# Decoding fp64 weight words by their bits, with the order of the decode's steps and one sum of every third pair placed on other engines

## The chip, the cores and the metric

The kernel runs on one core of one Trainium2 chip. The metric is the device time of one execution in microseconds; times that are compared are medians of several executions. Five queues matter: TensorE (PE, with its weight loads PEld), VectorE (DVE), ScalarE (ACT), GpSimd (POOL) and SyncE (SP), which issues nearly all DMAs. Each works through its own instructions in program order and waits at the head of its queue.

## What is computed

The reference, cut to what matters (12480 rows, 128 columns):

```python
h_filt = (np.maximum(pos_emb @ w1, 0) @ w2) * np.exp(-0.01 * pos)[:, None]
u = x * v
y = np.fft.irfft(np.fft.rfft(u, n=2 * S, axis=1) * np.fft.rfft(h_filt, n=2 * S, axis=0), n=2 * S, axis=1)[:, :S]
x = x * y
x = relu(x @ w_in) ** 2 @ w_out          # 128 -> 2048 -> 128
h = x @ w_in2
x = where(h > 0, h, exp(min(h, 0)) - 1) @ w_out2
```

The four weight matrices come as fp64 words. The kernel loads them as pairs of 32-bit words and makes fp32 numbers of them on the chip, each then split into a high part (fp32r) and the rest, since the matmuls of the last stage are done as three fp32r products.

## The kernel before

The program has three stages. **Stage one** (to 83 us of the profiled execution) makes the filter and the first of two transform steps. **Stage two** (`phase2`, 83 to 220 us) walks over 46 pairs p = 0 to 45 of transform rows. **Stage three** (`phase3`, from 220 us on) runs the two feed-forward layers over 25 column tiles, with 12 matmuls of 512 columns at a time.

A pair p of stage two goes through these steps, written in program order by the loop over p at the end of `phase2`:

- `s2(p)`: four matmul records on PE into the tile u (L503). There are two u buffers in PSUM.
- `prod(p)`: the complex product of u with the filter tile hh. VectorE makes the two product tiles (L515 into pt, L516 into m2). GpSimd makes the difference (L518, in place in pt) and the sum (L519, from m2 into pt). For p >= 43 (`PD - 1`) VectorE makes both.
- `s2r` on even p (L362, tile rt, copied to rr by ACT) and `hmm` on odd p (L375, tile h, copied to hh by ACT): the filter's part for later pairs. `hmm` reads rr, `prod` reads hh.
- `ia(p - 2)`: two matmul records on PE from pt into v (L526), an ACT copy into z, and a DMA of z to DRAM. It therefore waits for GpSimd's sum of the pair two before.

The weights are decoded beside this by a generator, `weights`, that is advanced four times per pair (once for p = 0). There are 16 chunks c of 128 x 512 words. `decode(c)` issues an instruction or nothing at each advance; a decode starts no earlier than advance 10 c (`WDEC`) and only when the one before has ended. It has nine advances before: bits of the mantissa (L417) and of the exponent (L419) on VectorE, three ACT conversions (L422, L424, L426), the low word added in (L428) and the sign put in (L430) on VectorE, and a 128 x 512 product of mantissa and power of two on GpSimd (L436). After L430 the DMA of chunk c + 2 into the same raw buffer is issued on SP. `split(c)`, at least four advances after its decode, copies the word to fp32r on ACT (L168, `m<-wf`) and subtracts on GpSimd (L165, `m<-wf,m`).

At the end of stage two, `head` makes the first column tile. For p = 44 and 45 it uses pt directly (L580), then needs the z rows of all earlier pairs. The z rows of pairs 40 to 43 are copied one by one by SP (`z0`, L537); VectorE copies and combines them (L583, L658), PE multiplies (L638, which waits for L583), and the first matmul of stage three follows.

Of the kernel before, what the change touches and what calls it, by code (L numbers as in the profile page):

```python
# [10 lines left out]
F32 = mybir.dt.float32  # L11
F32R = mybir.dt.float32r
U32 = mybir.dt.uint32
AF = mybir.ActivationFunctionType
ALU = mybir.AluOpType
SYNC = mybir.DependencyInfo(mybir.DependencyClass.Sync, mybir.DependencyReason.DATA)
# [25 lines left out]
PD = NP - 2  # L42
# [2 lines left out]
KD = K1 - 2 * PD  # L45
WDEC = 10
OFF = 3
LO0 = 8
LAG1 = 2
NX = 10  # L50
# [9 lines left out]
def _tiles():  # L60
    seq = [(p, s) for p in range(CEN + 1) for s in (1, -1) if p or s == 1]
    out = []
    b = 0
    for g in SIZES:
        part = seq[b:b + g]
        right = [p for p, s in part if s == 1]
        left = [p for p, s in part if s == -1]
        if not out:
            part = [(p, 1) for p in right] + [(p, -1) for p in left]
        out.append((right, left, [R if s < 0 and CEN - p < SPLIT else R - 1 for p, s in part], part))  # L70
        b += g
    assert b == len(seq)
    return out


def _fill():
    tl = _tiles()
    left = sum(tl[NT][2])
    out, b = [], 0
    for t in range(NT):  # L80
        n = 0 if t < FILL else min(FULL - sum(tl[t][2]), left - b)
        out.append((b, b + n))
        b += n
    assert b == left
    return out
# [69 lines left out]
class Build:  # L155
# [11 lines left out]
    def copy(self, out, in_):  # L167
        self.nc.scalar.activation(out=out, in_=in_, func=AF.Copy)  # L168

    def setup(self):  # L170
        nc = self.nc
        const = self.const = self.pool("const")
        self.dram = self.pool("dram", 1, DRAM)
        self.zero = const.tile([128, 128], F32, name="zero")
        nc.vector.memset(self.zero, 0.0)
        self.ebias = const.tile([128, 3], F32, name="ebias")
        self.sg = const.tile([128, 3], F32, name="sg")
        nc.vector.memset(self.ebias[:, 0:1], 1151.0)
        nc.vector.memset(self.ebias[:, 1:2], 255.0 * 8388608.0)
        self.Z = self.dram.tile([K1, 128, 2 * D], F32, name="Zd")  # L180
        self.wp = self.pool("wp")
        self.tiles = _tiles()
        self.fill = _fill()
        self.st = {}
# [30 lines left out]
    def phase1(self):  # L215
        nc, a = self.nc, self.a
        with ExitStack() as ctx1:
# [58 lines left out]
            def zstep(s):  # L276
                f = fb[s % 2]
                for c in range(2):
# [11 lines left out]
                    for h in range(2):  # L290
                        for n in range(4):
                            nc.scalar.activation(out=f[:, 0, h, n], in_=z[:, h, n], func=AF.Relu,
                                                 scale=win[:, s, 0, h, n:n + 1])
# [105 lines left out]
    def load_weights(self, c):  # L399
        l, k, q = c // 8, c // 4 % 2, c % 4  # L400
        raw = self.buf("raw", [4, D, 2], 2, U32, self.p2b)
        src = self.a[(("moe_w_in", "moe_w_out"), ("moe2_w_in", "moe2_w_out"))[l][k]].bitcast(U32)
        if k == 0:
# [6 lines left out]
    def decode(self, c):  # L410
        nc = self.nc
        raw = self.raw.pop(c)
        low, high = raw[:, :, :, 0], raw[:, :, :, 1]
        e = self.buf("we", [4, D], 2, U32, self.p2b)
        f = self.buf("wf", [4, D], WF, pool=self.p2b)
        t, s, w, m = e.bitcast(F32), e, f, f.bitcast(U32)
        nc.vector.tensor_scalar(out=m, in0=high, scalar1=0xFFFFF, scalar2=None, op0=ALU.bitwise_and)  # L417
        yield
        nc.vector.tensor_scalar(out=e, in0=high, scalar1=1, scalar2=21,  # L419
                                op0=ALU.logical_shift_left, op1=ALU.logical_shift_right)  # L420
        yield
        nc.scalar.activation(out=f, in_=m, func=AF.Copy, scale=2.0 ** -20, bias=1.0)  # L422
        yield
        nc.scalar.activation(out=t, in_=e, func=AF.Relu, bias=self.ebias[:, 0:1], scale=-1.0)  # L424
        yield
        nc.scalar.activation(out=e, in_=t, func=AF.Relu, bias=self.ebias[:, 1:2], scale=-8388608.0)  # L426
        yield
        nc.vector.scalar_tensor_tensor(out=f, in0=low, scalar=2.0 ** -52, in1=f, op0=ALU.mult, op1=ALU.add)  # L428
        yield
        nc.vector.scalar_tensor_tensor(out=s, in0=high, scalar=0x80000000, in1=e,  # L430
                                       op0=ALU.bitwise_and, op1=ALU.bitwise_or)
        if c + 2 < 16:
            self.load_weights(c + 2)
        yield
        yield
        nc.gpsimd.tensor_tensor(out=w, in0=f, in1=s.bitcast(F32), op=ALU.mult)  # L436
        yield
        self.dec[c] = w

# [36 lines left out]
    def phase2(self):  # L476
        nc, a, st = self.nc, self.a, self.st
        ctx0 = self.ctx
        with ExitStack() as self.ctx:
# [29 lines left out]
            def prod(p):  # L509
                nj = self.nj(p)  # L510
                u = st.pop(("u", p))[:, :nj]
                h = st.pop(("h", p))[:, :nj]
                pt = m1 = self.buf("pt", [2, 2, D], 5, pool=p2b)[:N2, :nj]
                m2 = self.buf("m2", [2, 2, D], 2, pool=p2b)[:N2, :nj]
                nc.vector.tensor_tensor(out=m1, in0=u, in1=h, op=ALU.mult)  # L515
                nc.vector.tensor_tensor(out=m2, in0=u, in1=h[:, :, ::-1], op=ALU.mult)  # L516
                eng = nc.vector if p >= PD - 1 else nc.gpsimd
                eng.tensor_tensor(out=pt[:, :, 0], in0=m1[:, :, 0], in1=m1[:, :, 1], op=ALU.subtract)  # L518
                eng.tensor_tensor(out=pt[:, :, 1], in0=m2[:, :, 0], in1=m2[:, :, 1], op=ALU.add)  # L519
                st["p", p] = pt  # L520

# [74 lines left out]
            for p in range(NP):  # L596
                self.pair = p
                if p in HD:
                    next(hd)
                if p < PD:  # L600
                    s2(p)
                if p:
                    next(wgen, None)
                prod(p)
                if p % 2 == 0 and p + 2 < NP:
                    self.s2r(p // 2 + 1)
                if p:
                    next(wgen, None)
                if p % 2 == 1 and p + 1 < NP:
                    self.hmm((p + 1) // 2)  # L610
                if PD <= p + 1 < NP:
                    s2(p + 1)
                if p:
                    next(wgen, None)
                if 1 < p <= PD:
                    ia(p - 2)
                if p == PD:
                    ia(p - 1)
                next(wgen, None)
# [43 lines left out]
    def phase3(self):  # L663
        nc, a = self.nc, self.a
        ctx0 = self.ctx
        with ExitStack() as self.ctx:
# [81 lines left out]
            def mm1(t, l, u, odd=False):  # L748
                n, ne = width(t)
                xh, xl = xin[t, l]  # L750
                w = self.w[l, 0]
                if odd:
                    hs = spare()
                elif l == 0:
                    hs = psh.tile([128, 2, 512], F32, tag="h", name="h")
                else:
                    hs = pair.pop("s")
                self.mm6([hs[:, b, :ne] for b in range(2)], w[:, 2 * u:2 * u + 2], [xh[:, :ne]] * 2, [xl[:, :ne]] * 2,
                         True, True)
                return hs[:, :, :ne]  # L760

            def pairs(pool, nm, t, dt=F32):
                return pool.tile([128, 2, 512], dt, tag=nm, name=nm)[:, :, :width(t)[1]]

            def lo_of(st, nm, eng, parts=(slice(0, 2),), after=None):
                lo = pairs(gh, nm, st["t"], F32R) if "lo" not in st else st["lo"]
                for b in parts:
                    i = self.sub(eng, lo[:, b], st["g"][:, b], st["hi"][:, b].bitcast(F32))
                    if after is not None:
                        self.tc.add_manual_dep(i.ins, after.ins.name, SYNC, reason="lo beside the reads of h")  # L770
                st["lo"] = lo
# [48 lines left out]
            def mid(k, own):  # L820
# [4 lines left out]
                e = two[k] = {"t": t2, "h": mm1(t2, 1, u2), "tn": pairs(gp, "tn", t2), "ex": pairs(gh, "ex", t2)}  # L825
                nc.scalar.activation(out=e["tn"], in_=e["h"], func=AF.Tanh, scale=0.5)  # L826
                nc.scalar.activation(out=e["ex"], in_=e["h"], func=AF.Exp)  # L827
# [12 lines left out]
            preps = {(0, 3): 1, (1, 0): NT, (1, 3): 2, **{(t, 0): t + 1 for t in range(2, NT - 1)}}  # L840
            LEAD = 8 + OFF
            for s in range(NS + LEAD + 2):
# [45 lines left out]
                if s - 1 in one:  # L888
                    lo_of(one[s - 1], "lo0", nc.gpsimd if s > LO0 else nc.vector, after=after)
                if both and t == 3:  # L890
# [76 lines left out]
```

## Time and profile before

| | us |
|---|---|
| median of 3 runs (1355.21 to 1355.42) | 1355.29 |
| the profiled execution | 1353.99 |
| its span, first to last instruction | 1352.2 |
| PE busy in the span | 1337.2 |
| VectorE, ACT, GpSimd busy | 1180.1, 1119.6, 644.9 |

The profiled execution's own time is 1.3 us below the median, and 1.8 us of it lie outside the span. PE is shown as busy almost throughout, but matmul ends are modelled, so the stage's pace has to be read from start times and from the waits. The granted clock of PE is 1.00 in every slice, which is the 2.4 GHz level.

### The profile page before, as it was taken

Reading aid. Unit: us, or ns where it says so; the run is one execution under the profiler, and the core shown is the slowest. Engines: PE = TensorE matmul, PEld = TensorE weight load, DVE = VectorE, ACT = ScalarE, POOL = GpSimd, SP = SyncE. Lnnn points to the kernel's source line nnn. Section 1 sums busy time; section 2 is a strip of 40 time slices with the busy share of each in tenths; the row PEclk is TensorE's granted clock in tenths of the full one; section 3 lists DMA queues with packets and bytes.
Section 4 is the critical chain, followed back from the end, with each engine's and each line's share of the span. In section 5 each row is a group of like instructions: output and inputs, shape, how many; then the busy total and the mean of one; then the engine's idle time right before and its main releaser. Section 6 shows DMA issues by size and latency. Waiting matters only on the chain.

```text
span 1352.2 us, 18781 instructions
## 1 busy us (share of the span) xinstructions
PE 1337.2 (99%) x6958; PEld 1114.2 (82%) x6958; DVE 1180.1 (87%) x1191; ACT 1119.6 (83%) x1435; POOL 644.9 (48%) x380
## 2 busy tenths in 40 slices
PE   9999999999999999999999999999999999999998
PEld 9987667898888888888888888888888888888885
DVE  6759996889989998998899888989898989898997
ACT  6778775788988898888888888988898889888885
POOL 3039992445744444444444444444444445444531
PEclk9999999999999999999999999999999999999999
DMA  8746775401110110011011101110111011100000
GB/s 263 220 141 209 215 228 149 135 4 51 52 38 16 53 52 26 28 53 52 13 40 52 53 1 52 53 52 2 52 53 49 4 53 53 35 2 9 8 8 14
DMA packets 71337, 89.35 MB, mean 66 GB/s; under 512 B 5579, under 2 KB 62790, under 8 KB 71246
## 3 DMA queue, kind: packets, MB, share of 16 engines
q1 hardware_dynamic: 71102, 88.03, 21.8%
q8 instruction: 55, 0.90, 0.3%
q14 instruction: 36, 0.29, 0.1%
q10 hardware_dynamic: 144, 0.13, 0.0%
HBM read 69.78 MB, written 18.32 MB: 65 GB/s over the span
## 4 chain that ended last, share of the span: by engine, by line
PE 91%; DVE 3%; POOL 2%; issue 1%; DMA 1%; ACT 1%; SPq 0%; DVEq 0%; POOLq 0%; ACTq 0%
PE h L193 38%; PE y L193 38%; PE s L317 4%; PE u L503 2%; PE v L526 2%; PE h L644 2%; PE h L648 2%; PE h L375 1%; PE rt L362 1%; PE s L283 1%; DVE g L898 1%; DVE lo L165 1%; POOL m L165 1%; POOL pt L518 1%; POOL pt L519 1%
## 5 line engine op out<-in xcount | busy, mean ns | idle before, releaser
L165 POOL TENSOR_TENSOR lo<-g,hi 128x1024 fp32r<-128x1024 f32 (+2 forms) x192 | 467.6, 2436 | 598.2 <-DVE tn L886 496.0
L193 PE MATMUL h<-xh,m 128*128 128x512 f32 (+3 forms) x1600 | 421.3, 385 | 3.4 <-DVE g L898 2.3
L193 PE MATMUL y<-hi,m 128*128 128x512 f32 (+2 forms) x1568 | 418.9, 389 | 0.0
L193 PEld LDWEIGHTS h<-xh,m 128*128 128x128 f32 x1600 | 298.7, 188 | 62.4 <-DVE g L898 3.4
L193 PEld LDWEIGHTS y<-hi,m 128*128 128x128 f32 x1568 | 290.0, 188 | 59.2 <-ACT ys L168 4.7
L886 DVE SCALAR_TENSOR_TENSOR tn<-ex,tn 128x1024 f32<-128x1024 f32 (+3 forms) x200 | 240.4, 1202 | 99.8 <-ACT ex L827 98.7
L826 ACT ACTIVATE tn<-h 128x1024 f32<-128x1024 f32 (+3 forms) x200 | 201.5, 1008 | 151.5 <-PE h L193 151.5
L165 DVE TENSOR_TENSOR lo<-ex,hi 128x1024 fp32r<-128x1024 f32 (+3 forms) x192 | 248.5, 1294 | 0.0
L898 DVE SCALAR_TENSOR_TENSOR g<-h,r 128x1024 f32<-128x1024 f32 (+3 forms) x200 | 238.4, 1192 | 9.2 <-ACT r L894 9.2
L193 PE MATMUL y<-lo,m 128*128 128x512 f32 (+2 forms) x784 | 240.4, 387 | 2.1 <-POOL lo L165 1.7
L193 PE MATMUL h<-xl,m 128*128 128x512 f32 (+3 forms) x800 | 242.1, 384 | 0.0
L912 DVE SCALAR_TENSOR_TENSOR ex<-tn,h 128x1024 f32<-128x1024 f32 (+3 forms) x200 | 237.1, 1185 | 1.4
L905 ACT ACTIVATE hi<-r 128x1024 fp32r<-128x1024 f32 (+3 forms) x200 | 209.8, 1049 | 0.5
L894 ACT ACTIVATE r<-h 128x1024 f32<-128x1024 f32 (+3 forms) x200 | 202.4, 1012 | 8.3 <-PE h L193 6.9
L168 ACT ACTIVATE hi<-ex 128x1024 fp32r<-128x1024 f32 (+2 forms) x192 | 203.9, 1062 | 0.0
L827 ACT ACTIVATE ex<-h 128x1024 f32<-128x1024 f32 (+3 forms) x200 | 199.6, 998 | 0.0
L193 PEld LDWEIGHTS y<-lo,m 128*128 128x128 f32 x784 | 146.5, 188 | 34.6 <-POOL lo L165 3.7
L193 PEld LDWEIGHTS h<-xl,m 128*128 128x128 f32 x800 | 149.5, 188 | 28.5
L518 POOL TENSOR_TENSOR pt<-pt 127x256 f32<-127x256 f32 x43 | 37.3, 868 | 69.6 <-DVE pt L515 69.1
L526 PE MATMUL v<-pt,g 127*128 127x512 f32 (+1 forms) x92 | 48.7, 615 | 2.3 <-DVE pt L515 2.3
L515 DVE TENSOR_TENSOR pt<-u,hh 127x512 f32<-127x512 f32 (+1 forms) x46 | 31.1, 676 | 20.3 <-PE u L503 19.7
L723 DVE SCALAR_TENSOR_TENSOR v<-z,sg 118x384 f32<-118x384 f32 (+3 forms) x75 | 43.0, 573 | 0.0
(89 smaller groups left out, 1086.1 us busy)
## 6 DMA issues: line engine op xcount, KB each, us to landing
Zd<-z SPq DMA_DIRECT2D x45, 256.0 KB
z<-Zd SPq DMA_DIRECT2D x48, 192.0 KB
z<-Zd SPq DMA_DIRECT2D x48, 136.5 KB
xc<-in_xv_dram SPq DMA_DIRECT2D x16, 392.0 KB
tb<-in_tf_dram SPq DMA_DIRECT2D x46, 127.0 KB
out_dram<-ys SPq DMA_DIRECT2D x22, 256.0 KB
raw<-in_moe_w_in_dram SPq DMA_DIRECT2D x8, 512.0 KB
raw<-in_moe_w_out_dram SPq DMA_DIRECT2D x8, 512.0 KB
```

Of the source, the lines that this page charges most:

```text
L165: return eng.tensor_tensor(out=out, in0=a, in1=b, op=ALU.subtract)
L168: self.nc.scalar.activation(out=out, in_=in_, func=AF.Copy)
L193: self.nc.tensor.matmul(outs[b], lhsT=w[:, b, h], rhs=x[b], start=first and i in ((0,) if one else (0, 2)), stop=last and i in ((5,) if on ...
L317: nc.tensor.matmul(pv[b:e, j // 2, :, j % 2], lhsT=fb[j][q], rhs=self.t1[:, :, q:q + 2], start=(j % 2 == 0), stop=(j % 2 == 1))
L526: nc.tensor.matmul(v, lhsT=self.g[:N2], rhs=pt.rearrange("p j r d -> p (j r d)"), start=True, stop=True)
L826: nc.scalar.activation(out=e["tn"], in_=e["h"], func=AF.Tanh, scale=0.5)
L827: nc.scalar.activation(out=e["ex"], in_=e["h"], func=AF.Exp)
L886: after = nc.vector.scalar_tensor_tensor(out=pa["em"], in0=pa["ex"], scalar=1.0, in1=pa["tn"], op0=ALU.add, op1=ALU.mult)
L894: nc.scalar.activation(out=f["r"], in_=f["h"], func=AF.Relu)
L898: nc.vector.scalar_tensor_tensor(out=f["g"], in0=f["h"], scalar=0.0, in1=f["r"], op0=ALU.max, op1=ALU.mult)
L905: nc.scalar.activation(out=f["hi"], in_=f["r"], func=AF.Square)
L912: nc.vector.scalar_tensor_tensor(out=pa["g"], in0=pa["em"], scalar=0.0, in1=pa["h"], op0=ALU.min, op1=ALU.max)
```

## The change

The decode gives up the split into mantissa and exponent. The high word is read as an fp32 number; ACT takes its absolute value (Abs), GpSimd clamps it between 2^-15 and a largest number (one `tensor_scalar` with max and min), and VectorE moves its bits into place by a shift left and right. ACT makes the last three mantissa bits from the upper half of the low word (Relu with scale and bias, then Copy into an integer). VectorE puts these bits in (`tensor_tensor`, bitwise or) and then the top two bits of the high word (`scalar_tensor_tensor`). The decode has ten advances instead of nine. In `prod`, the sum of a pair with p % 3 == 1 is made by VectorE (14 pairs below 43).

```diff
+TOP = float(np.array(0x47EFFFFF, np.uint32).view(np.float32))
-        nc.vector.memset(self.ebias[:, 0:1], 1151.0)
-        nc.vector.memset(self.ebias[:, 1:2], 255.0 * 8388608.0)
+        nc.vector.memset(self.ebias[:, 0:1], 7.0)
-        t, s, w, m = e.bitcast(F32), e, f, f.bitcast(U32)
-        nc.vector.tensor_scalar(out=m, in0=high, scalar1=0xFFFFF, scalar2=None, op0=ALU.bitwise_and)
-        yield
-        nc.vector.tensor_scalar(out=e, in0=high, scalar1=1, scalar2=21,
+        t, q, w = raw.bitcast(U16)[:, :, :, 1], f.bitcast(U32), f.bitcast(U32)
+        x = e.bitcast(F32)
+        nc.scalar.activation(out=x, in_=high.bitcast(F32), func=AF.Abs)
+        yield
+        nc.scalar.activation(out=f, in_=t, func=AF.Relu, bias=self.ebias[:, 0:1], scale=-2.0 ** -13)
+        yield
+        nc.gpsimd.tensor_scalar(out=x, in0=x, scalar1=2.0 ** -15, scalar2=TOP, op0=ALU.max, op1=ALU.min)
+        yield
+        nc.scalar.activation(out=q, in_=f, func=AF.Copy, scale=-1.0, bias=7.0)
+        yield
+        yield
+        nc.vector.tensor_scalar(out=e, in0=e, scalar1=5, scalar2=2,
                                 op0=ALU.logical_shift_left, op1=ALU.logical_shift_right)
         yield
-        nc.scalar.activation(out=f, in_=m, func=AF.Copy, scale=2.0 ** -20, bias=1.0)
-        yield
-        nc.scalar.activation(out=t, in_=e, func=AF.Relu, bias=self.ebias[:, 0:1], scale=-1.0)
-        yield
-        nc.scalar.activation(out=e, in_=t, func=AF.Relu, bias=self.ebias[:, 1:2], scale=-8388608.0)
-        yield
-        nc.vector.scalar_tensor_tensor(out=f, in0=low, scalar=2.0 ** -52, in1=f, op0=ALU.mult, op1=ALU.add)
-        yield
-        nc.vector.scalar_tensor_tensor(out=s, in0=high, scalar=0x80000000, in1=e,
+        nc.vector.tensor_tensor(out=e, in0=e, in1=q, op=ALU.bitwise_or)
+        yield
+        yield
+        nc.vector.scalar_tensor_tensor(out=w, in0=high, scalar=0xC0000000, in1=e,
                                        op0=ALU.bitwise_and, op1=ALU.bitwise_or)
         if c + 2 < 16:
             self.load_weights(c + 2)
         yield
-        yield
-        nc.gpsimd.tensor_tensor(out=w, in0=f, in1=s.bitcast(F32), op=ALU.mult)
+        w = f
         yield
         self.dec[c] = w
...
                 eng.tensor_tensor(out=pt[:, :, 0], in0=m1[:, :, 0], in1=m1[:, :, 1], op=ALU.subtract)
+                eng = nc.vector if p >= PD - 1 or p % 3 == 1 else nc.gpsimd
                 eng.tensor_tensor(out=pt[:, :, 1], in0=m2[:, :, 0], in1=m2[:, :, 1], op=ALU.add)
```

The change moves instructions in three places. Lines of the changed kernel count three or four higher: its L518, L519 are the products, L521 and L523 the difference and the sum, L167 and L170 the subtraction and the copy helpers.

VectorE at the end of stage two, before, from the last decode (the pair at its third row is p = 40) to the products of p = 42:

```order
L428 SCALAR_TENSOR_TENSOR wf_2231<-raw_2112,wf_2231 128x512
L430 SCALAR_TENSOR_TENSOR we_2230<-raw_2112,we_2230 128x512
L515 TENSOR_TENSOR pt_2278<-u_2274,hh_2264 127x512
L516 TENSOR_TENSOR m2_2279<-u_2274,hh_2264 127x512
L515 TENSOR_TENSOR pt_2300<-u_2297,hh_2264 127x512
L516 TENSOR_TENSOR m2_2301<-u_2297,hh_2264 127x512
L515 TENSOR_TENSOR pt_2327<-u_2323,hh_2315 127x512
L516 TENSOR_TENSOR m2_2328<-u_2323,hh_2315 127x512
```

The same engine in the changed kernel, from the products of p = 43 (pt_2326) to those of p = 44 (pt_2356):

```order
L518 TENSOR_TENSOR pt_2326<-u_2323,hh_2287 127x512
L519 TENSOR_TENSOR m2_2327<-u_2323,hh_2287 127x512
L521 TENSOR_TENSOR pt_2326<-pt_2326 127x2x128
L523 TENSOR_TENSOR pt_2326<-m2_2327 127x2x128
L428 TENSOR_SCALAR we_2298<-we_2298 128x512
L431 TENSOR_TENSOR we_2298<-we_2298,wf_2299 128x512
L434 SCALAR_TENSOR_TENSOR wf_2299<-raw_2203,we_2298 128x512
L518 TENSOR_TENSOR pt_2356<-u_2343,hh_2341 127x512
L519 TENSOR_TENSOR m2_2357<-u_2343,hh_2341 127x512
```

The last decode's instructions on VectorE moved from ahead of pair 40 to between pairs 43 and 44.

GpSimd near the end of stage two, before (the first pair shown is p = 38, pt_2217):

```order
L165 TENSOR_TENSOR m2_2025<-wf_1986,m2_2025 128x512
L436 TENSOR_TENSOR wf_2146<-wf_2146,we_2145 128x512
L518 TENSOR_TENSOR pt_2217<-pt_2217 127x2x128
L519 TENSOR_TENSOR pt_2217<-m2_2218 127x2x128
L165 TENSOR_TENSOR m2_2025<-wf_2063,m2_2025 128x512
L518 TENSOR_TENSOR pt_2248<-pt_2248 127x2x128
L519 TENSOR_TENSOR pt_2248<-m2_2249 127x2x128
L165 TENSOR_TENSOR m2_2025<-wf_2146,m2_2025 128x512
```

GpSimd in the changed kernel, from p = 38 (pt_2189) to its last instruction of the decode:

```order
L521 TENSOR_TENSOR pt_2189<-pt_2189 127x2x128
L523 TENSOR_TENSOR pt_2189<-m2_2190 127x2x128
L521 TENSOR_TENSOR pt_2215<-pt_2215 127x2x128
L523 TENSOR_TENSOR pt_2215<-m2_2216 127x2x128
L423 TENSOR_SCALAR we_2221<-we_2221 128x512
L521 TENSOR_TENSOR pt_2246<-pt_2246 127x2x128
L167 TENSOR_TENSOR m2_1999<-wf_2141,m2_1999 128x512
L521 TENSOR_TENSOR pt_2271<-pt_2271 127x2x128
L523 TENSOR_TENSOR pt_2271<-m2_2272 127x2x128
L521 TENSOR_TENSOR pt_2301<-pt_2301 127x2x128
L523 TENSOR_TENSOR pt_2301<-m2_2302 127x2x128
L423 TENSOR_SCALAR we_2298<-we_2298 128x512
```

The product L436 is gone, a clamp L423 stands in each decode, pair 40 (pt_2246) has no sum here, and the last two subtractions of the split come after the last pair.

## Rows read from the trace of the kernel before

**Rows 1.** A stretch of stage two: us, then busy us by engine, clock, DMA

```profile
125.00:164.00 39.00, 38.21 (x249) 27.56 (x248) 36.49 (x50) 28.90 (x47) 37.83 (x39) 1.00 0.68 207
```

**Rows 2.** Timeline of PE, stage two: start us, duration us, instruction, [idle before]

```profile
137.65 1.13 PE L526 MATMUL v<-pt,g 127*128 127x512 f32 x2
...
141.32 1.12 PE L526 MATMUL v<-pt,g 127*128 127x512 f32 x2 [0.79 <-DVE pt L515]
142.28 1.03 PE L503 MATMUL u<-m,tb 127*127 127x256 f32 x4
...
144.32 1.12 PE L526 MATMUL v<-pt,g 127*128 127x512 f32 x2
...
194.89 1.13 PE L526 MATMUL v<-pt,g 127*128 127x512 f32 x2
...
199.25 1.13 PE L526 MATMUL v<-pt,g 127*128 127x512 f32 x2 [1.48 <-DVE pt L515]
...
202.25 1.13 PE L526 MATMUL v<-pt,g 127*128 127x512 f32 x2
```

**Rows 3.** Timeline of VectorE and GpSimd ahead of PE's two waits

```profile
140.21 1.06 POOL L519 TENSOR_TENSOR pt<-m 127x256 f32<-127x256 f32 x1
...
192.10 0.68 DVE L516 TENSOR_TENSOR m<-u,hh 127x512 f32<-127x512 f32 x1
...
196.88 1.18 POOL L518 TENSOR_TENSOR pt<-pt 127x256 f32<-127x256 f32 x1
198.14 1.06 POOL L519 TENSOR_TENSOR pt<-m 127x256 f32<-127x256 f32 x1
```

**Rows 4.** Groups on GpSimd: instruction, count, busy us, mean ns, idle before

```profile
L519 POOL TENSOR_TENSOR pt<-m 127x256 f32<-127x256 f32 x43 | 37.8, 878 | 3.4
...
L436 POOL TENSOR_TENSOR wf<-wf,we 128x512 f32<-128x512 f32 x16 | 21.5, 1341 | 0.0
...
L744 POOL CAST xl<-rl 128x22 fp32r<-128x22 f32 (+3 forms) x23 | 4.5, 197 | 0.0
```

**Rows 5.** Instructions on tile raw: ns min/median/max, first and last start

```profile
L417 DVE TENSOR_SCALAR wf<-raw x16: 418/599/1480, 87.3 to 192.7; 128x512 uint32<-128x512 uint32 x16
L419 DVE TENSOR_SCALAR we<-raw x16: 417/950/1495, 87.8 to 193.6; 128x512 uint32<-128x512 uint32 x16
L428 DVE SCALAR_TENSOR_TENSOR wf<-raw,wf x16: 742/1249/1799, 89.3 to 195.7; 128x512 f32<-128x512 uint32 x16
L430 DVE SCALAR_TENSOR_TENSOR we<-raw,we x16: 818/1109/1220, 91.3 to 197.4; 128x512 uint32<-128x512 uint32 x16
```

**Rows 6.** Group of a VectorE operation with two SBUF inputs, stage three

```profile
L165 DVE TENSOR_TENSOR xl<-at,xh 128x490 fp32r<-128x490 f32 (+3 forms) x24 | 15.8, 657 | 0.0
```

**Rows 7.** Timeline of VectorE, pairs 43 (first two) and 44

```profile
206.72 0.69 DVE L515 TENSOR_TENSOR pt<-u,hh 127x512 f32<-127x512 f32 x1 [1.08 <-PE u L503]
...
208.46 0.83 DVE L519 TENSOR_TENSOR pt<-m 127x256 f32<-127x256 f32 x1
209.21 0.68 DVE L515 TENSOR_TENSOR pt<-u,hh 127x512 f32<-127x512 f32 x1
...
210.41 0.41 DVE L518 TENSOR_TENSOR pt<-pt 127x256 f32<-127x256 f32 x1
210.85 0.42 DVE L519 TENSOR_TENSOR pt<-m 127x256 f32<-127x256 f32 x1
```

**Rows 8.** Timeline of PE from the last pairs to the tile's product

```profile
206.97 0.93 PE L375 MATMUL h<-w,rr 64*127 64x128 f32 x12 [0.28 <-ACT rr L168]
...
210.09 2.83 PE L526 MATMUL v<-pt,g 127*128 127x512 f32 x6
...
217.50 2.03 PE L638 MATMUL h<-hx,xr 88*128 88x98 f32 x16 [0.17 <-DVE xr L583]
```

**Rows 9.** Timeline of ACT, the same place

```profile
205.90 0.63 ACT L168 ACTIVATE m<-wf 128x512 fp32r<-128x512 f32 x1 [1.89 <-POOL wf L436]
206.44 0.47 ACT L168 ACTIVATE rr<-rt 128x381 f32<-128x381 f32 x1
```

More of the change, by code (lines that the diff above doesn't have):

```diff
@@ L13 @@
 U32 = mybir.dt.uint32
+U16 = mybir.dt.uint16
 AF = mybir.ActivationFunctionType
```

## The prediction

> **What bounds the kernel now.** I read the page's busy times first, then a stretch of stage two (the only stage whose instructions change), then the start times on PE there, and last the queues that end PE's waits. PE is busy nearly throughout, so a shorter decode pays only where PE waits for it. In stage two three engines look full: PE 38.21 of 39 us, VectorE 36.49, GpSimd 37.83 [rows 1]. Busy shares don't tell which of the three sets the pace; the start times do. The v of an odd pair starts at 144.32 and, nine double pairs later, at 194.89 [rows 2]: 50.57 / 9 = 5.62 us for two pairs, 2.81 for one. The steps between keep this period to a hundredth whatever the others do, so it is PE's own pace. It is broken twice: 144.32 - 137.65 = 6.67 and 202.25 - 194.89 = 7.36 us [rows 2], which is 1.05 and 1.74 us too long, together 2.8 us.
>
> Both breaks are waits of v(p) for the pt of its pair. The row blames VectorE's L515, but GpSimd's sum L519 ends at 140.21 + 1.06 = 141.27 and at 198.14 + 1.06 = 199.20, and v starts 0.05 us later both times (141.32, 199.25) [rows 2, 3]. Counted along the queues these are the sums of pairs 18 and 38, which v needs. VectorE was through with pair 38 at 192.10 + 0.68 = 192.78; GpSimd began it at 196.88 [rows 3], 4.1 us behind. So GpSimd's backlog costs PE 2.8 us, and PE itself costs the rest.
>
> A third, small loss stands at the end: `hmm` waits 0.28 us for rr, which ACT makes right after a split copy that had waited 1.89 us for GpSimd's product L436 [rows 8, 9]. All waits for GpSimd together are worth 2.8 + 0.3 = 3.1 us, and nothing in stage two can give more, since PE does the same work in the same order.
>
> **GpSimd, part by part.** The change takes away 16 products of 1.34 us (21.5 us) and 14 sums of 0.88 us (12.3 us) [rows 4], together 33.8 us, and adds 16 clamps. No row shows a clamp, or any operation on GpSimd with one input of this size. Its ends are 0.20 us, what a copy of 22 columns takes, and 1.34 us for the same 512 columns with two inputs [rows 4]. I take 0.8, nearer to the row of the same size, less one input; that adds 13 us (3 to 21). If the two operations of the clamp ran one after the other at the two-input price it would be 2.7 us each; that is a rival. For the lower end speaks a page: the Trainium skill, GPSIMD Engine Reference, section 4.1 (Engine selection), says that one-input operations run at roughly line rate there and that it is the two-input ones that are slow, and its section 3.1 gives 1.03 cycles per element for a light loop, with section 1's 1.2 GHz an estimate of 0.44 us; no run here shows it, and by it the clamps would add 7 us instead of 13. So GpSimd sheds 13 to 31 us, about 21, of a load that fills 97% of the stretch [rows 1]. The backlog of 4 us can't build up any more, and I book both breaks, 2.8 us, as gone. The split copy on ACT no longer waits for GpSimd, but for VectorE's last decode step, several advances earlier: 0.3 us gone.
>
> **VectorE, part by part.** Before, a decode has four instructions with medians 0.60, 0.95, 1.25 and 1.11 us [rows 5], 3.9 us, 63 us for 16. After, three: a shift on the form of L419 (0.95), an or with two SBUF inputs, and a closing step on the form of L430 (1.11). The or lies between 0.66 us, a two-input operation of nearly that size [rows 6], and 1.25, the median of L428; I take 1.0. Sum 3.1 us, 49 us for 16. The 14 sums cost 0.42 to 0.83 each [rows 7], 6 to 12 us. VectorE thus sheds 2 to 8 us in total and is no tighter than before. Its worst burst is a sum, a shift, an or and a closing step between two pairs' products, 3.5 to 3.9 us; with 1.2 us for the products (209.21 to 210.41) [rows 7] that is 4.7 to 5.1 against the 2.81 of a pair, so it falls behind by 1.9 to 2.3 us. PE needs pt(p) only with v(p), which follows the u of two pairs later by 144.32 - 142.28 = 2.0 us [rows 2]: from start of u(p) that is 5.6 + 2.0, less 1.0 for u itself, 1.2 for the products and 1.5 for difference and sum, which leaves some 3.9 us. The burst is covered; its cover is gone if GpSimd is late by over 1.6 us at the same pair.
>
> **ACT and SP at nothing.** ACT keeps three operations per decode of the same size, hidden under PE's pace as before. The raw DMA still follows the closing step, 13 or 14 advances (9 to 10 us) before its chunk is read; SP's tb loads and z stores queue behind that wait as they do now.
>
> **The end of stage two, where the change costs.** A decode of ten advances makes starts come every 11 advances instead of 10, so the 16th comes 15 advances, nearly four pairs, later. The instruction order shows it: the last decode's three VectorE instructions move from ahead of pair 40 to between pairs 43 and 44. Before, VectorE has no decode left there and yet no slack: from 206.72 to the end of pair 44's sum at 210.85 + 0.42 = 211.27 it works without a pause [rows 7]. PE's third v from 210.09, v(44), starts two thirds into the 2.83 us [rows 8], about 211.9: slack 0.6. What is put between, at their shortest 0.42 + 0.66 + 0.82 = 1.9 us, is about 1.7 by start-to-start, and at their medians 3.1 [rows 5, 6]. GpSimd is nearly done by then, so I take a value near the short end, 1.9 (ends 1.7 and 3.1). It pushes v(44) by 1.9 - 0.6 = 1.3 us against pair 43. From v(44) on PE is busy through L580 to L638, which before waits only 0.17 us for the copied z rows [rows 8]; so L638 comes 1.3 - 0.2 = 1.1 us later against pair 43 (ends 0.9 and 2.3). The z rows themselves hang on v(41) to v(43) and SP, not on pair 44, and come earlier with them.
>
> **Sum.** Pair 43 comes 2.8 us earlier, the tail takes 1.1 back: -1.7 us, ends -0.5 and -1.9. Stage three keeps its order and starts as much earlier. Against the profiled execution that is 1353.99 - 1.7 = 1352.3 and a span of 1350.5. The median shown lies 1.3 above that execution, so the median forecast is 1355.29 - 1.7 = 1353.6.
>
> **The rivals.**
> *The tail is free.* If VectorE gets the last decode done while it waits for u, as it waits 1.08 us before pair 43 [rows 7], all 3.1 us stay: 1352.2, faster by 0.23%. For it: that idle time exists. Against: the order puts the three behind pair 43, and u(44) is there when they start. It needs the insertion to cost under 0.9 us.
> *The breaks only move.* GpSimd's clamp now stands ahead of a VectorE step, and VectorE waits at its head when GpSimd is late after a split of some 1.4 us; new breaks of 0.3 us at five of the sixteen decodes would eat 1.5 us: 1355.1, ends 1354.8 and 1356. For it: both queues stay at about four fifths or more. Against: the 3.9 us of cover above.
> *GpSimd becomes the bound, slower.* The clamp's price decides, and 33.8 / 16 = 2.1 us each is where GpSimd has its old load. Each tenth above costs 1.6 us; at 2.7 us (both operations at the two-input price) that is 9 us plus the tail's 1.1, some 1365, and from 2.3 us each it is slower by more than the bound below. For it: only that no row shows the price. Against: the nearest row of that size, 1.34.
> *VectorE becomes the bound, slower.* L428 takes 0.74 us at its shortest and 1.80 at its longest, L419 0.42 and 1.50 [rows 5], and the long ones lie beside GpSimd's instructions. If all forms ran near their longest (1.50, 1.25, 1.22 and sums of 0.83), the decodes would take 64 us and the sums 12, with 46 x 1.2 = 55 for the products: 131 us in a stage of 45 x 2.81 = 126, so some 5 us slower, 1360. Against: a GpSimd with 20 us less to do leaves more short forms. The Trainium skill, SBUF — State Buffer, "Who interferes with whom", states such a rule: a VectorE instruction with two SBUF inputs and a GpSimd one that reads SBUF exclude each other for the whole instruction. By it the or and the 14 sums are instructions of the blocking kind; the spread between shortest and longest agrees [rows 5].
>
> **How the numbers follow.** A difference within 0.2% (2.7 us) is about what a measurement of this kernel can tell from no change. Forecast 0.53 (1353.4 to 1354.8, same). Tail free 0.16 (1352.2, faster). Breaks move 0.18 (1354.8 to 1356, same). GpSimd the bound 0.07 and VectorE the bound 0.06 (slower). So faster 0.16, same 0.71, slower 0.13. The range reaches from 1351.9 to 1356.0: it holds the first three cases and leaves the slower two, 0.13, out.
>
> **What would show it.** Right: the two breaks of the 5.62 us period at pairs 18 and 38 gone, GpSimd about 21 us less busy in stage two, the clamp at 0.4 to 1.3 us, the last decode's three instructions on VectorE between pairs 43 and 44 with v(44) waiting 1 to 2 us for its sum, and L638 near 215.8 instead of 217.5. Wrong: new waits of v or u for VectorE in the middle of the stage, a clamp over 2 us, v(44) on time, or a stage three that does not start earlier by what L638 gains.

## The result and the profile after

| | before | after |
|---|---|---|
| median of 4 runs each, side by side | 1355.25 | 1374.03 |
| lowest, highest | 1353.91, 1355.42 | 1373.46, 1374.63 |
| the profiled execution, its span | 1353.99, 1352.2 | 1374.63, 1372.8 |

The ratio is 1.0141 (interval 1.0123 to 1.0158): the changed kernel is slower by 18.8 us. The forecast was 1353.6.

The place is plain from start times. The z-row matmuls that close stage two stood at 217.50 before [rows 8]; now they start at 238.22, 20.7 us later, of which stage one gave 0.6 (the first u at 84.66 instead of 84.04). The first matmul of stage three is 20.6 us later, and so is the end of the span (1372.8 - 1352.2), so stage three only shifts. All that follows is stage two.

GpSimd's groups of the changed kernel, 80 to 240 us (line, engine, operation, tiles, shapes, count | busy us, mean ns | idle before it and for whom); they answer to [rows 4]:

```profile
L521 POOL TENSOR_TENSOR pt<-pt 127x256 f32<-127x256 f32 x43 | 31.4, 731 | 97.2 <-DVE pt L518 96.8
L423 POOL TENSOR_SCALAR we<-we 128x512 f32<-128x512 f32 x16 | 30.7, 1917 | 0.0
L523 POOL TENSOR_TENSOR pt<-m 127x256 f32<-127x256 f32 x29 | 24.4, 842 | 2.3
L167 POOL TENSOR_TENSOR m<-wf,m 128x512 fp32r<-128x512 f32 x16 | 22.1, 1384 | 2.5 <-ACT m L170 2.5
```

Their sum is 108.6 us, where the four groups before made 119.3 (37.8 + 37.3 + 22.7 + 21.5). GpSimd has less to do, and the stage is 20 us longer. It isn't GpSimd's capacity, then. The waits say what it is. The waits of the changed kernel, 85 to 220 us (who waited for whom: us in total, times, longest):

```profile
POOL pt L521 <- DVE pt L518: 96.8, 22, 65.3
...
DVE pt L523 <- POOL pt L521: 19.9, 14, 4.8
...
DVE we L428 <- POOL we L423: 13.5, 7, 3.2
...
PE u L506 <- DVE m L519: 7.6, 7, 2.0
```

Two new kinds of wait stand on VectorE, together over 33 us: the sum L523 waits for GpSimd's difference L521 in each of its 14 pairs, and the shift L428 waits for GpSimd's clamp L423. GpSimd in turn waits more for VectorE's products: 96.8 us, of which 65.3 are the idle time of stage one, so 31.5; before it was 69.1 with the same 65.3, so 3.8. Two engines that each wait for the other lose time that neither lacks.

One such knot, read across three engines. GpSimd of the changed kernel from 113 us on (start, us, engine, line, operation, tiles, shapes, count, and in brackets the idle time before it and its releaser):

```profile
113.82 0.73 POOL L523 TENSOR_TENSOR pt<-m 127x256 f32<-127x256 f32 x1
114.51 1.92 POOL L423 TENSOR_SCALAR we<-we 128x512 f32<-128x512 f32 x1
116.39 1.28 POOL L167 TENSOR_TENSOR m<-wf,m 128x512 fp32r<-128x512 f32 x1
117.62 0.74 POOL L521 TENSOR_TENSOR pt<-pt 127x256 f32<-127x256 f32 x1
118.32 1.27 POOL L167 TENSOR_TENSOR m<-wf,m 128x512 fp32r<-128x512 f32 x1
122.41 0.73 POOL L521 TENSOR_TENSOR pt<-pt 127x256 f32<-127x256 f32 x1 [2.82 <-DVE pt L518]
...
125.40 1.92 POOL L423 TENSOR_SCALAR we<-we 128x512 f32<-128x512 f32 x1
```

VectorE of the same kernel, the same stretch and columns:

```profile
112.94 0.67 DVE L519 TENSOR_TENSOR m<-u,hh 127x512 f32<-127x512 f32 x1
118.40 1.47 DVE L523 TENSOR_TENSOR pt<-m 127x256 f32<-127x256 f32 x1 [4.79 <-POOL pt L521]
119.79 0.41 DVE L428 TENSOR_SCALAR we<-we 128x512 uint32<-128x512 uint32 x1
...
121.65 0.68 DVE L518 TENSOR_TENSOR pt<-u,hh 127x512 f32<-127x512 f32 x1
122.25 0.68 DVE L519 TENSOR_TENSOR m<-u,hh 127x512 f32<-127x512 f32 x1
...
127.35 0.43 DVE L428 TENSOR_SCALAR we<-we 128x512 uint32<-128x512 uint32 x1 [3.23 <-POOL we L423]
```

And PE, from 120 us on and at the end of the stage:

```profile
120.02 1.10 PE L530 MATMUL v<-pt,g 127*128 127x512 f32 x2 [1.35 <-DVE pt L523]
123.08 2.04 PE L506 MATMUL u<-m,tb 127*127 127x256 f32 x4 [1.96 <-DVE m L519]
...
231.19 1.63 PE L530 MATMUL v<-pt,g 127*128 127x512 f32 x2 [4.34 <-DVE pt L523]
...
238.22 1.92 PE L642 MATMUL h<-hx,xr 88*128 88x98 f32 x16
```

VectorE is through with its products at 113.61 and comes to the sum. The sum may not write yet: its output pt[:, :, 1] is the second half of the first product, which GpSimd's difference still has to read (`pt = m1`, and the difference is made in place). GpSimd has a sum, a clamp and a split before that difference, and ends it at 118.36; VectorE has stood 4.79 us. In that time VectorE makes no products, so GpSimd, after one more split, stands 2.82 us itself. Then VectorE reaches the next shift before GpSimd has begun the clamp, and stands 3.23 us. PE gets its v 1.35 us late and, since `s2` needs a u buffer that the products free, its u 1.96 us late. PE's waits in stage two add up to 14.7 us (1.35, 1.96, 0.35, 1.95, 0.56, 0.25, 1.24, 1.44, 1.30, 4.34), against 0.79 + 1.48 + 0.28 = 2.55 before [rows 2, 8]: 12.2 us more.

A further part isn't waiting. Windows of the changed kernel (stretch, its length, then busy time and count of PE, PEld, VectorE, ACT and GpSimd, the granted clock, DMA share, GB/s):

```profile
120.00:124.00 4.00, 2.02 (x4) 1.12 (x5) 3.86 (x7) 1.23 (x2) 1.51 (x3) 0.80 0.22 39
124.00:128.00 4.00, 4.00 (x20) 2.62 (x19) 0.78 (x3) 0.82 (x1) 3.23 (x3) 0.50 0.86 289
...
212.00:216.00 4.00, 4.00 (x16) 3.20 (x16) 2.26 (x4) 1.16 (x3) 3.83 (x5) 0.68 0.59 196
...
232.00:236.00 4.00, 4.00 (x15) 3.48 (x15) 1.60 (x6) 0.60 (x1) 0.00 (x0) 0.62 0.31 103
```

Before, the granted clock is 1.00 in all of stage two. Now, after the pair of waits at 118.67 to 120.02 and 121.12 to 123.08, it is 0.50 for all of 124 to 128, the 1.2 GHz level: the u at 123.08 takes 2.04 us where the one at 116.75 takes 1.03. The same follows the waits near 208 and 231. Seven windows of 4 us up to 240 lie below 1.00; the clock lost in them, 4 us x (1 - clock) added up, is 6.8 us (0.80, 0.50, 0.85, 0.89, 0.68, 0.95, 0.62). That is an upper bound, since the windows also count the clock while PE stood; by start times the three slow stretches are 6.3 us longer than the same matmuls at the full clock. So 0.6 + 12.2 + 6.8 = 19.6 of the 20.7 us; the last 1.1, or 1.6 by start times, I can't assign.

### The profile page after: what moved, and what is told of

Its sections match the earlier page's. It is cut to its first block, busy times and chain, and to the rows that moved or that the text cites. A ratio compares the mean times of both kernels' runs of the same rounds, so it can differ in the third digit from the quotient of the medians.

```text
span 1372.8 us, 18802 instructions
## 1 busy us (share of the span) xinstructions
PE 1347.2 (98%) x6958; PEld 1120.3 (82%) x6958; DVE 1171.9 (85%) x1188; ACT 1119.9 (82%) x1435; POOL 635.3 (46%) x366
## 4 chain that ended last, share of the span: by engine, by line
PE 87%; DVE 5%; POOL 4%; issue 2%; DMA 1%; ACT 1%; SPq 0%; DVEq 0%; POOLq 0%; ACTq 0%
PE h L194 38%; PE y L194 37%; PE s L318 4%; PE h L648 2%; PE h L652 2%; POOL pt L521 1%; POOL we L423 1%; DVE pt L518 1%; PE s L284 1%; PE u L506 1%; POOL pt L523 1%; PE v L530 1%; DVE pt L523 1%; PE y L786 1%; PE h L376 0%
## 5 line engine op out<-in xcount | busy, mean ns | idle before, releaser
L167 POOL TENSOR_TENSOR lo<-g,hi 128x1024 fp32r<-128x1024 f32 (+2 forms) x192 | 467.8, 2437 | 598.9 <-DVE tn L890 495.9
L167 DVE TENSOR_TENSOR lo<-ex,hi 128x1024 fp32r<-128x1024 f32 (+3 forms) x192 | 248.0, 1291 | 0.0
L170 ACT ACTIVATE hi<-ex 128x1024 fp32r<-128x1024 f32 (+2 forms) x192 | 203.8, 1062 | 0.0
L521 POOL TENSOR_TENSOR pt<-pt 127x256 f32<-127x256 f32 x43 | 31.4, 731 | 97.2 <-DVE pt L518 96.8
L506 PEld LDWEIGHTS u<-m,tb 127*127 127x127 f32 x128 | 24.2, 195 | 23.9 <-issue 14.0
```

What stands on the lines that cost most here:

```text
L167: return eng.tensor_tensor(out=out, in0=a, in1=b, op=ALU.subtract)
```

## The experiments

Times are medians beside the kernel before on the same chip, whose medians lay between 1354.1 and 1354.7. Differences between experiments that ran on different chips are taken between their distances from that kernel.

**Which of the two new waits is it?** First the changed kernel with its sums back on GpSimd:

```diff
-                eng = nc.vector if p >= PD - 1 or p % 3 == 1 else nc.gpsimd
```

> The changed kernel with all sums of pairs below 43 back on GpSimd; the new decode stays. Theory A (VectorE's sum overwrites the half of the product tile that GpSimd's difference has still to read, so VectorE stands at its queue's head for GpSimd 14 times, 19.9 us in the trace of the changed kernel): those waits vanish, GpSimd gets 14 x 0.84 = 12 us of work back and is about full (75 + 22 + 31 = 128 us in a stage of 126), so 1355 to 1361. Theory B (the clamp, 1.92 us instead of the 0.8 I took, and VectorE's 13.5 us of waits for it): with even more work on GpSimd the time stays at 1368 or more.

1374.03 us, ratio 1.0143 (1.0128 to 1.0158), the same as the changed kernel; Theory A's 1355 to 1361 is out. The sum's wait is gone, and the clamp's has grown to fill its place. Its waits, 85 to 220 us:

```profile
DVE we L428 <- POOL we L423: 37.7, 15, 4.5
```

Then the other part alone, the kernel before with only the sum of every third pair on VectorE:

```diff
+                eng = nc.vector if p >= PD - 1 or p % 3 == 1 else nc.gpsimd
```

> The kernel before with one edit: the sum of every third pair on VectorE; the old decode stays. Theory A: the same 14 waits for GpSimd's difference, now behind L436 and the split's subtraction: slower than before by 4 to 15 us, 1359 to 1370. Theory B: no clamp, and GpSimd has 12 us less to do, so the waits of PE at pairs 18 and 38 go: 1352 to 1355.

1361.72 us, 1.0051 (1.0034 to 1.0068): slower by 7.0 us, without any clamp. Its waits, 85 to 220 us:

```profile
ACT wf L422 <- DVE wf L417: 19.0, 13, 3.2
...
DVE pt L520 <- POOL pt L518: 12.7, 14, 2.6
```

Each part of the change slows the kernel by itself, 19.3 us and 7.0 us, and together they give 18.8. Waits of one queue don't add: whoever stands at the sum finds the clamp done. VectorE's two kinds of wait make 33.4 us in the changed kernel, and the clamp's alone 37.7 once the sum's are gone.

**The dependence turned round.** The changed kernel with VectorE making the difference and GpSimd the sum of those pairs, so that GpSimd waits for VectorE and not the other way:

```diff
-                eng = nc.vector if p >= PD - 1 else nc.gpsimd
+                eng = nc.vector if p >= PD - 1 or p % 3 == 1 else nc.gpsimd
                 eng.tensor_tensor(out=pt[:, :, 0], in0=m1[:, :, 0], in1=m1[:, :, 1], op=ALU.subtract)
-                eng = nc.vector if p >= PD - 1 or p % 3 == 1 else nc.gpsimd
+                eng = nc.vector if p >= PD - 1 else nc.gpsimd
                 eng.tensor_tensor(out=pt[:, :, 1], in0=m2[:, :, 0], in1=m2[:, :, 1], op=ALU.add)
```

> The changed kernel, but for every third pair VectorE makes the difference (in place) and GpSimd the sum: the same number of instructions of the same size on each engine, only that now GpSimd waits for VectorE and no longer VectorE for GpSimd. Theory A: 14 waits gone with nothing else changed, 1354 to 1359. Theory B: the clamp and its waits are as they were, 1368 or more. Theory C (the extra instruction on VectorE and the shared way into SBUF cost the time, not the wait): 1370 or more.

1374.95 us, 1.0148 (1.0133 to 1.0163): with the clamp in place this gains nothing (the shift waits 31.4 us in 16 waits). The same edit to the kernel before, which has no clamp:

> The kernel before with one edit: for every third pair VectorE makes the difference instead of GpSimd; GpSimd keeps the sum. Against the run that moved the sum instead (1361.7) it has the same number of instructions of the same size on each engine; only the wait is turned round (GpSimd waits for VectorE). Wait theory: the 14 waits of VectorE (12.7 us) vanish and GpSimd has 12 us less to do: 1352 to 1356. Theory C (the sum cost 7 us because VectorE is full): about 1361 again.

1353.65 us, 0.9997 (0.9987 to 1.0006). Against e2_sum_only VectorE does as many instructions of the same size, and 7.5 us lie between them (7.0 above and 0.5 under the kernel before). One more run separates wait from load: e2_sum_only, with the first product of those pairs in a tile of its own, so that the sum overwrites nothing:

```diff
                 pt = m1 = self.buf("pt", [2, 2, D], 5, pool=p2b)[:N2, :nj]
+                if p < PD - 1 and p % 3 == 1:
+                    m1 = self.buf("m1", [2, 2, D], 2, pool=p2b)[:N2, :nj]
```

> The kernel before with the sum of every third pair on VectorE, as in e2_sum_only (1361.7, +7.0 us), but with one thing taken away: for those pairs the first product goes into a tile of its own instead of pt, so that GpSimd's difference reads that tile and the sum overwrites nothing that the difference still has to read. Theory (the 7 us of e2 are VectorE's waits at the sum, 12.7 us in 14 waits, which exist only because the sum overwrites the second half of the first product): the waits of the sum for GpSimd's difference vanish, no further wait takes their place, and the time is at the kernel before or up to 1.5 us under it, 1353 to 1355. Rival (VectorE's added load, 14 sums, or the collision of its sums with GpSimd's instructions costs the 7 us): the waits may vanish, the time stays near 1361. A third outcome: the sum still waits, since it writes into the same tile as the difference does; then the time stays near 1361 too, with the waits in place, and the run tells nothing on the first two.

1357.17 us, 1.002 (1.001 to 1.0029). This is outside the theory's 1353 to 1355. The sum no longer waits for the difference at all, and 4.3 of the 7.0 us are gone: that much was the overwritten half. 2.7 us stay. They aren't VectorE's load as such, since it is busy 126.22 us from 84 to 220 here and 125.92 in e9_before_difference_on_vectore, which loses nothing. What differs is ACT's wait for VectorE's first decode step (L422 for L417), 13.7 us here, 19.0 in e2_sum_only, 5.6 in e9, and the rr copies behind it, for which PE then waits up to 1.33 us. Why the sum delays that step and the difference does not is left open.

**The clamp off GpSimd.** The changed kernel with the clamp on VectorE, its sums on GpSimd:

```diff
-        nc.gpsimd.tensor_scalar(out=x, in0=x, scalar1=2.0 ** -15, scalar2=TOP, op0=ALU.max, op1=ALU.min)
+        nc.vector.tensor_scalar(out=x, in0=x, scalar1=2.0 ** -15, scalar2=TOP, op0=ALU.max, op1=ALU.min)
...
-                eng = nc.vector if p >= PD - 1 or p % 3 == 1 else nc.gpsimd
```

> As the first of these (sums on GpSimd), and the clamp on VectorE too, so that no VectorE instruction waits for GpSimd anywhere and GpSimd has 75 + 22 = 97 us. Theory A: no wait of PE for GpSimd or VectorE is left but at the end of the stage, 1352 to 1355, and less than the first by what the full GpSimd costs there. Theory B: this one alone of the four is near 1353. If VectorE with four decode steps again becomes the bound: 1356 to 1360.

1355.07 us, 1.0003 (0.9994 to 1.0012): 19.0 us better than e1_sum_back by this one line. PE has no wait at all in stage two until the one that the prediction put at v(44). PE (its first u of stage two, then the end of the stage) and VectorE (the end) of this kernel:

```profile
83.36 1.13 PE L506 MATMUL u<-m,tb 127*127 127x256 f32 x4
...
211.19 1.10 PE L529 MATMUL v<-pt,g 127*128 127x512 f32 x2 [3.10 <-DVE pt L522]
...
216.54 1.93 PE L641 MATMUL h<-hx,xr 88*128 88x98 f32 x16
```

```profile
204.41 1.39 DVE L521 TENSOR_TENSOR pt<-pt 127x256 f32<-127x256 f32 x1
205.83 0.42 DVE L522 TENSOR_TENSOR pt<-m 127x256 f32<-127x256 f32 x1
206.17 0.42 DVE L428 TENSOR_SCALAR we<-we 128x512 uint32<-128x512 uint32 x1
...
208.03 0.68 DVE L518 TENSOR_TENSOR pt<-u,hh 127x512 f32<-127x512 f32 x1
...
209.68 1.37 DVE L522 TENSOR_TENSOR pt<-m 127x256 f32<-127x256 f32 x1
```

The three decode instructions take 208.03 - 206.17 = 1.86 us. But pair 43's difference takes 1.39 and pair 44's sum 1.37, where 0.42 is what the undisturbed ones take. GpSimd of the same kernel:

```profile
204.25 1.26 POOL L167 TENSOR_TENSOR m<-wf,m 128x512 fp32r<-128x512 f32 x1 [1.00 <-ACT m L170]
209.32 1.44 POOL L167 TENSOR_TENSOR m<-wf,m 128x512 fp32r<-128x512 f32 x1 [3.81 <-ACT m L170]
```

Both long ones lie beside a split that began before them and end 0.29 us after it: the difference at 205.80 and its split at 205.51, the sum at 211.05 and its split at 210.76. The splits have moved with the decode. The Trainium skill, SBUF — State Buffer, "Who interferes with whom", states that a VectorE instruction with two SBUF inputs and a GpSimd one that reads SBUF block each other whole; these two places agree.

The same with the sums left on VectorE, so the changed kernel with only the clamp moved:

> The changed kernel with the clamp on VectorE and every third pair's sum left on VectorE: against the earlier run with the clamp on VectorE and the sums on GpSimd (1355.1) it differs by the sums alone. Theory A (now: each wait of VectorE at the head of its queue for GpSimd costs, the clamp's more than the sum's): 14 waits for GpSimd's difference stay, but GpSimd has only pairs and splits, so they are short: 1355 to 1359. Theory C (a sum on VectorE is free where GpSimd has no decode work): 1354 to 1356.

1357.62 us, 1.0022 (1.0012 to 1.0031): 3.1 us above the kernel before, where the changed kernel is 18.8 above it. The sum's waits are 7.5 us then, and the kernel is 2.8 us slower than e4_clamp_on_vectore.

**The end of the stage.** e4_clamp_on_vectore with one of the decode's empty advances taken out, which makes nine of ten:

```diff
         nc.scalar.activation(out=q, in_=f, func=AF.Copy, scale=-1.0, bias=7.0)
         yield
-        yield
```

> Sums on GpSimd, clamp on VectorE, and one empty advance taken out of the decode, so that it has nine advances as before and the last decode's VectorE instructions stand ahead of pair 40 again; no instruction is added or removed against the run with ten advances (1355.1), whose PE waits 3.1 us for the pt of pair 44. Tail theory: that wait and the lower clock after it go, 1351 to 1352.5. If the wait at pair 44 is not due to the decode between pairs 43 and 44: no change, 1355.

1351.82 us, 0.9979 (0.9968 to 0.9989): the fastest of all, 2.7 us under the kernel before and some 21 under the changed one. PE of this kernel, its first u of stage two and then the end of the stage:

```profile
84.35 1.13 PE L505 MATMUL u<-m,tb 127*127 127x256 f32 x4
...
207.21 2.83 PE L528 MATMUL v<-pt,g 127*128 127x512 f32 x6
...
215.50 2.03 PE L640 MATMUL h<-hx,xr 88*128 88x98 f32 x16 [1.05 <-DVE xr L585]
218.65 1.67 PE L194 MATMUL h<-xh,m 128*128 128x392 f32 x4 [1.12 <-ACT xh L170]
```

v(44) doesn't wait any more. The z-row matmuls do, by 1.05 us, for VectorE's copy of the z rows, which waits 5.5 us for their DMA; this is the next wait of the stage. The lower clock that the expectation saw going did not go: it is 0.80 from 216 to 220 and 0.77 from 220 to 224, after these 1.05 us and the 1.12 behind them.

**What makes the clamp's wait.** Three kernels on the base of e3_roles_swapped. Half a clamp, on 256 of 512 columns:

> The kernel with roles swapped (1375) with the clamp on half of the columns only (256 of 512; the other half is left unclamped), so GpSimd's clamp takes about 1.0 us instead of 1.92. If the clamp's price sets the time (each of 16 waits of VectorE shortens by 0.9 us): 1359 to 1363. If the time is set by the place of the clamp in the queues, whatever it costs: 1368 or more.

The clamp with one operation (max) instead of two:

> The kernel with roles swapped (1375) with the clamp's lower bound only (max, no min; the upper bound is left out): a price row. If the two operations of the clamp cost one after the other, it falls from 1.92 us towards 1.0 and the time to about 1359, like the half clamp (1.07 us, 1359.3). If one pass costs the same with one operation or two: 1.9 us and 1375.

The whole clamp, issued at the end of the chunk before, six advances ahead of the shift instead of three:

> The kernel with roles swapped (1375), where each chunk's Abs and clamp are issued at the end of the decode before, so that six advances (4.2 us) instead of three (2.1 us) lie between the clamp on GpSimd and the shift on VectorE. The same instructions on each engine, the same clamp of 1.92 us, the last decode's VectorE instructions at the same place. Wait theory (VectorE's wait at its queue's head for the clamp is what costs): those waits go almost wholly, 1355 to 1360. Load theory (the clamp costs because GpSimd has too much to do): 1368 or more.

| kernel | clamp, median us | advances ahead | VectorE's wait for it, us | median, us |
|---|---|---|---|---|
| e3_roles_swapped | 1.91 | 3 | 31.4 | 1374.95 |
| e10_one_op_clamp | 1.49 | 3 | 23.1 | 1365.84 |
| e7_half_clamp | 1.06 | 3 | 16.2 | 1359.31 |
| e8_early_clamp | 1.91 | 6 | 15.4 | 1360.61 |
| e4_clamp_on_vectore (all sums on GpSimd) | (on VectorE) | | 0 | 1355.07 |

Ratios: 1.0078 (1.0063 to 1.0093), 1.0032 (1.002 to 1.0043) and 1.0043 (1.0026 to 1.0059) for the second, third and fourth. The half clamp came out as forecast, the one-operation clamp between its two cases. Both shorten the clamp and take load off GpSimd at once, so the fourth row is the one that decides. The tile of the clamp in e8_early_clamp (minimum, median and longest ns, first and last start; then what VectorE waited for it, in us and times):

```profile
L417 POOL TENSOR_SCALAR we<-we x16: 1911/1914/2133, 88.8 to 208.9; 128x512 f32<-128x512 f32 x16
...
  POOL we L417: 15.4, 11
```

Sixteen clamps at the same price, the same instructions on GpSimd, and the kernel is some 14 us faster, with half the waiting. GpSimd's instructions of stage two even take a little longer than in e3_roles_swapped (114.4 us against 111.3). The waits did not go almost wholly, as the wait theory had it, and the median lies 0.6 us above its range; but the load theory's 1368 or more is out. So the time goes by how long VectorE stands at the shift, which in the knot above is GpSimd's backlog plus the clamp less the lead, and not by what GpSimd has to do.

## Why the prediction was wrong

- **PE's own pace, and 3.1 us of waits for GpSimd: right.** In e4_clamp_on_vectore and e6_nine_advances both breaks of the 5.62 us period are gone, and no other wait is left in the stage until its end. The first u of the kernel before:

```profile
84.04 1.13 PE L503 MATMUL u<-m,tb 127*127 127x256 f32 x4
```

 Counted from the first u, the block of the last v starts at 207.21 - 84.35 = 122.86 in e6_nine_advances and at 210.09 - 84.04 = 126.05 before [rows 8]: 3.19 us earlier, where 3.1 were put on all waits for GpSimd.
- **"GpSimd, part by part" mis-sized the clamp.** Its tile in the changed kernel reads:

```profile
L423 POOL TENSOR_SCALAR we<-we x16: 1911/1916/1925, 89.0 to 223.3; 128x512 f32<-128x512 f32 x16
```

 It takes 1.92 us, not 0.8, and is above both ends (0.20 and 1.34). The upper end was wrong in kind: fewer inputs don't mean less time here, since the two-input split of the same size has a median of 1.27 us in this kernel. By the prediction's own terms GpSimd sheds 33.8 - 30.7 = 3.1 us and not 21; its groups together shed 10.7, as the differences ran shorter too. But that is still less load than before, as the rival "GpSimd becomes the bound" put it with its 2.1 us, and load isn't what cost the time. The estimate of 0.44 us from the Trainium skill (GPSIMD Engine Reference, sections 3.1 and 4.1) lies further off still; the measurement decides.
- **The step that failed: "The backlog of 4 us can't build up any more, and I book both breaks as gone".** It took the queues for loads. The change made VectorE wait for GpSimd in two places where before it hardly waited, and a backlog on GpSimd that used to reach PE only through pt now stops VectorE, whose products are what GpSimd and PE live on. GpSimd stops in turn (31.5 us of waits for VectorE's products, 3.8 before). The sum's dependence (its output is the second half of m1) wasn't in the prediction at all, though `pt = m1` stands in the code; alone it is 4.3 us of the 7.0 that e2_sum_only loses.
- **"VectorE, part by part": the load was right, the cover wrong.** The three decode instructions take 11.8 + 13.5 + 15.1 = 40.4 us (49 forecast), and all 16 full-size sums 14.0 (the 14 new ones were put at 6 to 12). That is less than VectorE had to do before. The cover of 3.9 us held for the burst of VectorE's own work, and the text said that it ends if GpSimd is late by over 1.6 us. The clamp alone takes longer than that, and in the knot above the difference stands behind a sum, a clamp and a split.
- **The rival "The breaks only move" was the mechanism, at under a tenth of its size.** It named the clamp at VectorE's head, but with 0.3 us at five decodes; the shift waits 31.4 us at all 16 in e3_roles_swapped. Three advances are 2.1 us at PE's pace (2.81 x 3 / 4), of which the clamp alone takes 1.9; one split ahead of it (1.3) uses up the lead. It also lacked the echo, GpSimd waiting for the VectorE that waits for it, and PE's clock after the waits, at most 6.8 us.
- **The end of stage two: place and insertion right, term mis-sized.** The last decode stands between pairs 43 and 44 and takes 1.86 us (1.9 forecast), but v(44) waits 3.10 us in e4_clamp_on_vectore, not 1.3. Of these, 1.05 would be spent at the z-row matmuls anyhow, as e6_nine_advances shows, where the prediction had 0.2. So the two traces, counted from the first u to the z-row matmuls, lie 133.18 - 131.15 = 2.0 us apart, and the medians beside the kernel before 3.05; forecast were 1.1. "GpSimd is nearly done by then" was wrong: its last splits moved too, and lengthened two of VectorE's instructions by some 0.95 each; 1.86 + 1.9 - 0.6 of slack makes 3.2, about the 3.10 measured. In the changed kernel v(44) waits 4.34 us: there the shift also waits 0.60 us for the clamp and then takes 1.49 beside a split.
- **Sum and range.** The gain that the sum booked is there once the new waits are taken out: e6_nine_advances, without them and without the tail, is 2.7 us under the kernel before (interval 1.5 to 4.3), where 2.8 were booked. With the tail, e4_clamp_on_vectore is at +0.4 (interval -0.8 to +1.6) and not at -1.7. The sum put VectorE's waits for GpSimd at nothing; they bring the 12.2 us of PE's waits (4.34 of them at v(44)) and the lower clock behind these. The range, to 1356.0, priced new waits at the size of the old ones.

## What to carry to other kernels

When a step moves to another engine, list the waits between in-order queues that it makes, tiles that are written in place included, and for each hold its lead against the producer's price plus its backlog; an engine with less to do can still stop its neighbour. Where two engines share work on one pair, let the one with slack wait for the one that others live on, give the producer a longer lead, or keep producer and consumer on one queue. Moving a short step (here the clamp) onto the engine that needs it can cost less than the wait, even if that engine is the busier one.

## What the runs showed of the hardware

- A GpSimd `tensor_scalar` on 128 x 512 fp32 words with max and min takes 1.92 us, with max alone 1.49, on 256 columns with both 1.06. The 1.92 is longer than a two-input subtraction of that size (median 1.27 in the changed kernel, 1.46 in the kernel before). On VectorE the same clamp has a median of 0.59 us (0.42 to 1.43).
- After PE waits of 1.35 and 1.96 us close together, the granted clock fell to the 1.2 GHz level (0.50 from 124 to 128), which doubled the matmul times there. Single waits of 2.40 us (e3_roles_swapped, to 121.35) and 2.49 us (e1_sum_back, to 199.30) were also followed by it: a u of 1.88 us and a v of 2.07, where 1.03 and 1.12 are usual. One of 1.95 us in the changed kernel (to 160.12) was not, the next u takes 1.10. In e4_clamp_on_vectore the granted clock is 1.00 from 212 to 216, right behind the 3.10 us at v(44), 0.96 from 216 to 220, where PE waits another 1.12 us, and 0.61 from 220 to 224.
